# Two attentions in one Trainium2 kernel: V by column tiles, the first K and Q in parts, PE warmed in one run, more clock-keeping matmuls early on

## The chip, the cores and the metric

The kernel runs on one core of one Trainium2 chip. The core has four engines that matter here, each with an instruction stream of its own, tied together by semaphores: TensorE (PE, with its weight loads PEld), VectorE (DVE), ScalarE (ACT) and GpSimd (POOL). SyncE (SP) issues DMAs. The metric is the device time of one execution in microseconds, as the median of several runs; lower is better.

## What is computed

Two independent layers read different inputs, and their outputs stand side by side in the last axis. Part A is attention of 16 query heads over one shared key and value head; part B is attention of 16 heads, each query over the 8 keys at distances 0, 2, ... 14 behind it.

```python
S, D, H, Dh = 2048, 448, 16, 28
# A: x (1,S,D), wq (D,D), wk and wv (D,Dh), wo (D,D)
q = (x @ wq).reshape(B, S, H, Dh).transpose(0, 2, 1, 3)
k = x @ wk;  v = x @ wv
p = softmax(einsum("bhqd,bkd->bhqk", q, k) * Dh ** -0.5)
a = einsum("bhqk,bkd->bhqd", p, v).transpose(0, 2, 1, 3).reshape(B, S, D) @ wo
# B: x (1,S,D), wqkv (D,3D), wo (D,D); W = 8, dil = 2
idx = pos[:, None] - 2 * arange(8)[None, :]
logits = einsum("bhsd,bhswd->bhsw", q, k[:, :, idx]) * Dh ** -0.5   # -1e9 where idx < 0
b = einsum("bhsw,bhswd->bhsd", softmax(logits), v[:, :, idx]).transpose(...).reshape(B, S, D) @ wo
out = concatenate([a, b], axis=-1)
```

## The kernel before

**Part A in units.** The queries are cut into four chunks of 512 (`sc`), the heads into four groups of four (`t`, head `j` of a group on 32 partitions of its own), the keys into 16 blocks of 128 (`tb`). A unit is one (sc, t, tb, j): scores of 128 keys by 512 queries. There are 1024 units, 64 to a (sc, t), which the code calls a quad (a "group" in the text below). PSUM banks 0 to 4 are a ring of two slots, one of three banks and one of two, so a round of both slots takes five units. For each slot PE makes the scores, ACT takes the exp of the whole slot in one instruction (1536 or 1024 columns, `expT`, L833), and PE multiplies four exps at a time with V (L879, output on 32 partitions for each j, bank 5). Scores have two forms: four heads' worth of 32-row tiles side by side (L816), or full 128-row matmuls against `kz`, a copy of K that is zero outside the rows of head j (L813).

In some rounds of each group one unit is not done by ACT: DVE computes its exp by a polynomial, a conversion for each unit (`d_x`, L912) and three steps for each pair of units (L921, L923, L925, 1024 columns each) that leave `dexp`. `OFF_AT` lists these rounds for each group.

**The head.** The first two chunks of x are loaded by ACT's queue in rows (`stage`, also `xst`) and transposed by PE (`a_tr`, L694) and copied to `xT_A` (L702 on DVE, L705 on ACT); the other two come by transposing DMAs (L608). From `xT_A` come K of each chunk (L660), Q of each group (L752) and V of each chunk (L716). K and Q carry their own squared norm: a Square of the projection (ACT L758 and L666 for the first, DVE L670/L672 and L762/L764 for the others), a matmul with `hq` that adds it (L674, L766), and an add of a column on DVE that leaves `kT` (L677) and `qT` (L770). V is scaled by `gcol`, an exp of a column of K (L723 on PE, L727 on ACT, L731 on DVE), and lands in `v_aug`, with its factor copied in by POOL (L729). Before all this PE runs `WARM` matmuls on zeros (L651) that nobody reads.

**Part B** works through 16 blocks of 128 queries (`b_qk` L1003, `b_v` L1018, `b_logits` L1044 and L1053, `b_soft`, `b_out` L1098 to L1114) with PSUM banks 6 and 7, which it shares with the later K, Q, V and with A's output projection (L962).

**The order is planned.** Every instruction is entered with an estimated duration, its reads and writes, a rank `pr` (lower goes first) and an earliest time `rel`, in planned microseconds. A list scheduler (`Sched.run`) walks the engines' clocks and always starts the ready instruction of the lowest rank; the result is a fixed order for each engine, with semaphore waits between engines. What it does not see is the true time: an engine that meets an unfulfilled wait stands, with all that is behind it.

```python
if limit is not None and not o.ring and not (o.pv and npv > self.NPV) and T + o.dur > limit + self.EPS - (0 if o.tiled else self.MODE):
    nxt = limit if nxt is None else min(nxt, max(limit, T + 0.02))
    continue
key = (o.pr, o.idx)
```

`limit` is the time when the next scores or conversion of the ring are due, so other work is only put where it fits ahead of them. The planner also counts the columns that PE got in the last `WIN` microseconds, `area(T)`, and where the count is low it adds matmuls on zeros, the clock-keeping matmuls (L413 in a free bank, L436 next to small matmuls, L808 in a ring slot), or gives scores their full form (L813). `WANT`, `IDLE`, `FULL` and `LOW` are the thresholds:

```python
elif (o.full and area(T) < (self.FULL[o.full] if T + 0.22 * o.full + 0.2 <= H + self.EPS else self.LOW)
      and all(d.start is not None and d.end + self.lat(d) <= T for d in o.opt)):
    o.dur = 0.22 * o.full
```

`H` is the planned time at which ACT runs out of exps.

## Time and profile before

| | us |
|---|---|
| median of 8 runs | 453.22 (452.18 to 456.26) |
| the profiled execution: its own time | 452.85 |
| its span, first to last instruction | 450.8 |
| busy in the span: ACT, PE, DVE | 435.3, 419.5, 417.1 |
| first exp of the ring starts | 11.72 |
| last exp ends (chain: 443.57 and 1.46 more) | 445.03 |
| granted TensorE clock, mean | 0.996 |

A row of the profile's groups has the line of the code, the engine, the operation, output and inputs by name with their shapes, the count, then busy time and mean duration in ns, and last the idle time of the engine just before such instructions with what ended it. A row of a timeline starts with the start and the length in us of the merged instructions. The chain is the work that ended last, followed backwards; its share of the span by engine says which engine sets the end. Durations of matmuls include their run through the array, so that back-to-back ones overlap in the record.

### The profile page before, as it was taken

How to read it: one execution, taken by the hardware profiler on the slowest of the kernel's cores; microseconds unless marked ns; L12 is line 12 of the kernel's file. 1: busy time of each engine (PE TensorE's matmuls, PEld its weight loads, DVE VectorE, ACT ScalarE, POOL GpSimd, SP SyncE). 2: the span in 40 equal slices, each digit the busy share in tenths (PEclk: the TensorE clock that was granted, in tenths of full speed). 3: DMA queues.
4: the chain of work that ended last, by engine and by line, in shares of the span. 5: the costliest groups of instructions: out<-in, count | busy, mean ns of one | idle time of the engine just before them, and what ended most of it. 6: DMA issues, size and time to landing. Idle time of an engine off the chain costs nothing.

```text
span 450.8 us, 9035 instructions
## 1 busy us (share of the span) xinstructions
PE 419.5 (93%) x3806; PEld 164.9 (37%) x3806; DVE 417.1 (93%) x672; ACT 435.3 (97%) x429; POOL 14.4 (3%) x37
## 2 busy tenths in 40 slices
...
PEclk9999999999999999999999999999999999999998
...
DMA packets 39988, 27.30 MB, mean 61 GB/s; under 512 B 15518, under 2 KB 39592, under 8 KB 39948
## 3 DMA queue, kind: packets, MB, share of 16 engines
...
q0 software_dynamic: 816, 1.53, 1.9%
...
q14 instruction: 10, 0.08, 0.1%
...
## 4 chain that ended last, share of the span: by engine, by line
ACT 91%; DVE 4%; PE 3%; DMA 1%; issue 0%
ACT expT L833 90%; DMA stage<-in_A_x_dram 1%; PE ps L660 1%; DVE kz L680 1%; DVE d_x L912 1%; ACT e_t L1079 1%; DVE d_u L921 1%; DVE d_u L923 1%; PE ps L694 0%; PE ps L813 0%; DVE qT L770 0%; DVE kT L677 0%; PE ps L436 0%; DVE xT_A L702 0%; PE ps L816 0%; DVE kT L670 0%
## 5 line engine op out<-in xcount | busy, mean ns | idle before, releaser
L833 ACT ACTIVATE expT<-ps 128x1024 bf16<-128x1024 f32 (+1 forms) x410 | 429.8, 1261 | 4.1 <-PE ps L816 1.9
L816 PE MATMUL ps<-qT,kT 32*128 32x512 bf16 (+1 forms) x918 | 130.4, 372 | 13.7 <-ACT expT L833 10.6
L879 PE MATMUL ps<-expT,v_aug 128*32 128x512 bf16 (+1 forms) x1000 | 89.8, 375 | 1.4 <-ACT expT L833 1.0
L816 PEld LDWEIGHTS ps<-qT,kT 32*128 32x128 bf16 x918 | 32.8, 91 | 101.7 <-ACT expT L833 87.0
L912 DVE TENSOR_SCALAR d_x<-ps 128x512 f32<-128x512 f32 x84 | 57.6, 685 | 2.1 <-PE ps L816 1.9
L813 PE MATMUL ps<-qT,kz 128*128 128x512 bf16 (+1 forms) x170 | 47.2, 368 | 7.1 <-ACT expT L833 5.5
L925 DVE SCALAR_TENSOR_TENSOR dexp<-d_u,d_x 128x1024 int16<-128x1024 f32 x42 | 51.3, 1221 | 0.1
L923 DVE SCALAR_TENSOR_TENSOR d_u<-d_u,d_x 128x1024 f32<-128x1024 f32 x42 | 51.2, 1220 | 0.1
L921 DVE SCALAR_TENSOR_TENSOR d_u<-d_x 128x1024 f32<-128x1024 uint16 x42 | 51.2, 1218 | 0.2
L1044 DVE TENSOR_TENSOR stage<-qTB,kTB 112x1024 bf16<-112x1024 bf16 x64 | 42.5, 681 | 1.0 <-PE ps L1053 0.9
L1104 PE MATMUL ps<-ident,prod 128*112 128x128 bf16 x512 | 42.2, 224 | 0.0
L1098 DVE TENSOR_TENSOR prod<-Vsh,a_n 128x896 bf16<-128x896 bf16 x64 | 37.7, 620 | 4.7 <-PE ps L1104 4.7
L1003 PE MATMUL ps<-xT_B,wqkv 128*128 128x512 bf16 x128 | 39.0, 384 | 0.7 <-DVE qT L770 0.4
L879 PEld LDWEIGHTS ps<-expT,v_aug 128*32 128x32 bf16 x1000 | 22.0, 93 | 47.9 <-issue 43.1
L1104 PEld LDWEIGHTS ps<-ident,prod 128*112 128x112 bf16 x512 | 34.0, 130 | 14.7 <-issue 11.7
L1053 PEld LDWEIGHTS ps<-ones,stage 112*128 112x128 bf16 x512 | 19.9, 96 | 9.2 <-issue 4.3
L1053 PE MATMUL ps<-ones,stage 112*128 112x4 bf16 x512 | 22.9, 167 | 0.0
L752 PE MATMUL ps<-xT_A,wq 128*128 128x512 bf16 x64 | 19.8, 385 | 0.3 <-DVE kTB L1008 0.2
L813 PEld LDWEIGHTS ps<-qT,kz 128*128 128x128 bf16 x170 | 10.9, 97 | 24.0 <-ACT expT L833 21.1
L1018 PE MATMUL ps<-wqv,xT_B 128*128 128x448 bf16 x64 | 18.1, 356 | 0.9 <-DVE kTB L1008 0.5
L1111 PE MATMUL ps<-wo_B,oT 112*128 112x448 bf16 x64 | 18.3, 357 | 0.0
L962 PE MATMUL ps<-wo,oTn 128*128 128x448 bf16 x64 | 16.6, 357 | 1.1 <-DVE oTn L948 1.1
...
## 6 DMA issues: line engine op xcount, KB each, us to landing
...
```

The lines of the kernel that those rows point to most:

```text
L813: r = e.matmul(g.bank(b0 + i, nq, nq * k), g.kz[:, j, 128 * tb:128 * tb + 128], g.qT[:, sc % 2, t, q0:q0 + nq], start=True, stop=True)
L816: r = e.matmul(g.bank(b0 + i, nq, nq * k), g.kT[32 * j:32 * j + 32, 128 * tb:128 * tb + 128], g.qT[32 * j:32 * j + 32, sc % 2, t, q0:q0 + ...
L833: x = a("act", t_exp(w), lambda e, b0=b0, w=w, n=n: e.activation(g.expT[:, n % ERING, 0:w], g.ps[:, 512 * b0:512 * b0 + w], ACT.Exp, scale ...
L879: x = e.matmul(g.bank(PVBANK, nq, q0, p0=32 * j, p1=32 * j + 32), g.v_aug[:, w, tb, :], src[:, nq * k:nq * k + nq], start=first, stop=last ...
L912: o = a("dve", t_dve_ps(512), lambda e: e.tensor_scalar(out=xx[:, 512 * h:512 * h + 512], in0=g.bank(bank), scalar1=-128.0 * A2, scalar2=1 ...
L921: a("dve", t_dve_1x(1024), lambda e: e.scalar_tensor_tensor(out=u, in0=lo, scalar=EP * F, in1=lo, op0=ALU.add, op1=ALU.mult), R=di, W=["d_ ...
L923: a("dve", t_dve_1x(1024), lambda e: e.scalar_tensor_tensor(out=v, in0=u, scalar=EQ * F * F, in1=lo, op0=ALU.add, op1=ALU.mult), R=["d_u"] ...
L925: a("dve", t_dve_1x(1024), lambda e: e.scalar_tensor_tensor(out=out, in0=v, scalar=EL / F ** 3, in1=xx, op0=ALU.mult, op1=ALU.subtract), R ...
L1003: a("pe", t_mm(512), lambda e, u=u, t=t, kt=kt, w=w: e.matmul(g.bank(u.bank), g.wqkv[:, kt, w * D + KC * t:w * D + KC * t + 128], g.xT_B[: ...
L1044: op = a("dve", t_dve_2x(1024), lambda e, t=t, qv=qv, kv=kv: e.tensor_tensor(out=g.prodT[0:KC, t, :, :], in0=qv, in1=kv, op=ALU.mult), R=R ...
L1053: r = e.matmul(g.bank(u.bank, 128).rearrange("p (h w) -> p h w", w=WIN)[:, 4 * t:4 * t + 4, w], g.prodT[0:KC, t, w, :], g.ones4[:, :], sta ...
L1104: a("pe", 0.056, lambda e, u=u, t=t, w=w: e.matmul(g.bank(u.bank, 128, 128 * t, p1=KC), g.prod2[:, w, KC * t:KC * t + KC], g.ident[:, :], ...
```

## The change

- The warming matmuls become one planned instruction of eight with the first rank of PE, and a ninth not before 4.6.
- K of chunk 0 and Q of the first group are made in two parts of 256 columns, each with a Square, a norm matmul and an add of its own. Scores of key blocks 0 and 1 need only the first part of K (`key_of`).
- V turns its operands round: `wv4` (32 columns wide) is the stationary side, x streams by in four column tiles at a time, and DVE transposes the result (`vT`) before the scaling. The `gcol` column goes into K's bank.
- The first group's DVE units come in rounds 4 to 7 instead of 7 to 10. The polynomial steps get a rank that grows with the group (`pp`: -25 for the first, 1.7 for the second, 26.7 more for each further one) in place of -1.5, and `d_x` has three buffers.
- The DVE steps of Q of the first chunk get rank -2.
- `area` counts 200 less between 14 and 50, and thresholds, weights and some durations of the plan are set anew.
- B starts not before 30; late loads are issued later (`wqv` 15, `wo_B` 40, `wo4` 44, the third and fourth chunk of `xT_B` 60 and 130); the rest of `wq` and the zero rows of V's scratch go earlier.

```diff
-WARM = 9
+WARM = 8
+KF = 256
...
-OFF_AT[0] = (7, 8, 9, 10)
+OFF_AT[0] = (4, 5, 6, 7)
 LATE = 2
-PSTT = -1.5
+PSTT = -35.0
 DR = 2
+DX = 3
...
-    MODE = 0.09
+    MODE = 0.096
...
-    WIN = 2.2
-    WANT = 1200.0
-    IDLE = 1300.0
-    FULL = {2: 1500.0, 3: 1200.0}
-    LOW = 900.0
-    QKT = 0.315
+    WIN = 2.5
+    WANT = 1300.0
+    IDLE = 1400.0
+    FULL = {2: 1400.0, 3: 1300.0}
+    LOW = 1200.0
+    QKT = 0.32
...
-            return sum(d for (t1, d) in recent if t1 > T - self.WIN) / self.WIN
+            return sum(d for (t1, d) in recent if t1 > T - self.WIN) / self.WIN - (200.0 if 14 < T < 50 else 0.0)
...
-                if ok and left > 40:
+                if ok and left > 10:
...
+                elif mode and not o.tiled:
+                    o.dur += o.extra
...
-        self.d_x = sb([128, 2, 1024], FP32, "d_x")
+        self.d_x = sb([128, DX, 1024], FP32, "d_x")
...
-        self.outA = sb([128, 4, D], BF16, "outA")
+        self.outA = sb([128, 2, D], BF16, "outA")
...
+        a("dve", 0.1, lambda e: e.memset(g.wv4[:, :, :], 0.0), W=["wv4z"], pr=-6.5)
...
-        a("gp", 0.5, lambda e: e.memset(g.Vst[:, 0, :], 0.0), W=[("Vst", 0)], pr=-8.05)
...
-        a("gp", 1.5, wload(g.wq, g.A_wq, KC, D), R=[("d_x", 0, 0), ("d_x", 0, 1)], W=[("wq", 1)], dsem="i_wq", land=4, pr=-7.5, ninc=2)
+        a("gp", 1.5, wload(g.wq, g.A_wq, KC, D), R=[("d_x", 0, 0), ("d_x", 0, 1)], W=[("wq", 1)], dsem="i_wq", land=5.5, pr=-8.15, ninc=2)
...
-                    transpose=True)), R=[("xst", 0)], W=[("xT", c, t)], dsem=f"i_xa{c}.{t}", land=3.8, pr=-20 + c)
+                    transpose=True)), R=[("xst", 0)], W=[("xT", c, t)], dsem=f"i_xa{c}.{t}", land=5.0 if c == 2 else 8.0, pr=-20 + c)
...
-                    transpose=True)), R=[("xst", 0)], W=[("xT_B", c, t)], dsem=f"i_xb{c}.{t}", land=4.5, pr=-16 + c)
+                    transpose=True)), R=[("xst", 0)], W=[("xT_B", c, t)], dsem=f"i_xb{c}.{t}", land=6.0, pr=-16 + c, rel=(0, 0, 60, 130)[c])
...
-          W=["wqv"], dsem="i_wbv", land=5, pr=-7, ninc=2)
+          W=["wqv"], dsem="i_wbv", land=8, pr=-7, rel=15, ninc=2)
...
-            for t in range(4)], W=["wo_B"], dsem="i_wob", land=5, pr=2, rel=4, ninc=4)
+            for t in range(4)], W=["wo_B"], dsem="i_wob", land=5, pr=2, rel=40, ninc=4)
...
-            for j in range(4)], W=["wo4"], dsem="i_wo4", land=5, pr=2, rel=4, ninc=4)
...
+            for j in range(4)], W=["wo4"], dsem="i_wo4", land=5, pr=2, rel=44, ninc=4)
+        a("sp", 0.6, one(lambda e: e.dma_start(out=g.v_dram[0:PAD, :], in_=g.warm[0:PAD, 0:D])),
+          R=["warm"], W=[("vd", -1)], dsem="i_vz", land=2.5, pr=-24)
...
+        a("dve", 0.1, lambda e: e.tensor_copy(out=g.wv4[:, :, 0:DH], in_=g.wv[:, :, :]), R=["wv", "wvz", "wv4z"], W=["wv4"], pr=-5)
...
+    VPR = 0.5
+    VP0 = 0.5
+    BREL = 30.0
...
-        for i in range(WARM):
-            u = Use(f"warm{i}", (3,))
-            a("pe", 0.33, lambda e, u=u: e.matmul(g.bank(u.bank), g.warm[:, 0:128], g.warm[:, :], start=True, stop=True),
-              R=["warm"], use=u, pr=-15)
+        for n, pr, rel in ((WARM, -30, 0.0), (1, -15, 4.6)):
+            def warm(e, n=n):
+                for _ in range(n):
+                    r = e.matmul(g.bank(3), g.warm[:, 0:128], g.warm[:, :], start=True, stop=True)
+                return r
+            u = Use(f"warm{n}", (3,))
+            a("pe", 0.43 * n, warm, R=["warm"], use=u, pr=pr, rel=rel)
         for c in range(NCH):
             pr = -9 if c == 0 else c
             HB = g.HB if c == 0 else g.LB
             if c < 2:
                 g.a_tr(c)
-            u = Use(f"K{c}", HB, late=c == 0)
-            for kt in range(4):
-                a("pe", t_mm(512), lambda e, u=u, c=c, kt=kt: e.matmul(
-                    g.bank(u.bank), g.wk4[:, kt, :], g.xT_A[:, kt, 512 * c:512 * c + 512],
-                    start=kt == 0, stop=kt == 3),
-                  R=[("xT", c, kt), "wk4"], W=[u], use=u, pr=pr, rel=8.0 * min(c, 1), dense=512)
-            ksq = g.k_sq[:, c % 2, :]
-            if c == 0:
-                a("act", t_act(512), lambda e, u=u, ksq=ksq: e.activation(ksq, g.bank(u.bank), ACT.Square),
-                  R=[u, "d_u"], W=[("k_sq", c % 2)], use=u, pr=-100)
-            else:
-                kc = g.kT[:, 512 * c:512 * c + 512]
-                a("dve", t_dve_ps(512), lambda e, u=u, kc=kc: e.tensor_copy(out=kc, in_=g.bank(u.bank)),
-                  R=[u], W=[("kT", c)], use=u, pr=min(pr, -2))
-                a("dve", t_dve_2x(512), lambda e, ksq=ksq, kc=kc: e.tensor_tensor(out=ksq, in0=kc, in1=kc, op=ALU.mult),
-                  R=[("kT", c), "d_u"], W=[("k_sq", c % 2)], pr=-2)
-            a("pe", t_mm(512), lambda e, u=u, ksq=ksq: e.matmul(g.bank(u.bank), g.hq[:, 2, :], ksq, start=False, stop=True, skip_group_check=True),
-              R=[("k_sq", c % 2), "hq", "d_u"], W=[u], use=u, pr=pr, dense=512)
+            for k, (lo, n) in enumerate(((0, KF), (KF, 512 - KF)) if c == 0 else ((0, 512),)):
+                u = Use(f"K{c}.{k}", HB, late=c == 0)
+                for kt in range(4):
+                    a("pe", t_mm(n), lambda e, u=u, c=c, kt=kt, lo=lo, n=n: e.matmul(
+                        g.bank(u.bank, n), g.wk4[:, kt, :], g.xT_A[:, kt, 512 * c + lo:512 * c + lo + n],
+                        start=kt == 0, stop=kt == 3),
+                      R=[("xT", c, kt), "wk4"], W=[u], use=u, pr=pr + 0.1 * k, rel=8.0 * min(c, 1), dense=n)
+                ksq = g.k_sq[:, c % 2, lo:lo + n]
+                kc = g.kT[:, 512 * c + lo:512 * c + lo + n]
+                if c == 0:
+                    a("act", t_act(n), lambda e, u=u, ksq=ksq, n=n: e.activation(ksq, g.bank(u.bank, n), ACT.Square),
+                      R=[u, "d_u"], W=[("k_sq", c % 2, k)], use=u, pr=-100)
+                else:
+                    a("dve", t_dve_ps(n), lambda e, u=u, kc=kc, n=n: e.tensor_copy(out=kc, in_=g.bank(u.bank, n)),
+                      R=[u], W=[("kT", c, k)], use=u, pr=min(pr, -2))
+                    a("dve", t_dve_2x(n), lambda e, ksq=ksq, kc=kc: e.tensor_tensor(out=ksq, in0=kc, in1=kc, op=ALU.mult),
+                      R=[("kT", c, k), "d_u"], W=[("k_sq", c % 2, k)], pr=-2)
+                a("pe", t_mm(n), lambda e, u=u, ksq=ksq, n=n: e.matmul(
+                    g.bank(u.bank, n), g.hq[:, 2, :], ksq, start=False, stop=True, skip_group_check=True),
+                  R=[("k_sq", c % 2, k), "hq", "d_u"], W=[u], use=u, pr=pr + 0.1 * k, dense=n)
+                a("dve", t_dve_ps(n) + 0.08, lambda e, u=u, kc=kc, n=n: e.tensor_scalar(
+                    out=kc, in0=g.bank(u.bank, n), scalar1=g.cols[:, 0:1], scalar2=None, op0=ALU.add),
+                  R=["kadd"], W=[("kT", c, k)], use=u, pr=min(pr, -2) - (1 - k if c == 0 else 0))
             kc = g.kT[:, 512 * c:512 * c + 512]
-            a("dve", t_dve_ps(512), lambda e, u=u, kc=kc: e.tensor_scalar(
-                out=kc, in0=g.bank(u.bank), scalar1=g.cols[:, 0:1], scalar2=None, op0=ALU.add),
-              R=["kadd"], W=[("kT", c)], use=u, pr=min(pr, -2))
-            g.kz_ops[c] = [a("dve", Lock(0.265), lambda e, j=j, c=c, kc=kc: e.tensor_scalar(
+            g.kz_ops[c] = [a("dve", Lock(0.3), lambda e, j=j, c=c, kc=kc: e.tensor_scalar(
                 out=g.kz[:, j, 512 * c:512 * c + 512], in0=kc, scalar1=g.cols[:, 8 + j:9 + j], scalar2=None, op0=ALU.mult),
-                R=["jmask", ("kT", c)], W=[("kz", c)], pr=4 + c) for j in range(4)]
+                R=["jmask"] + g.keys_of(c), W=[("kz", c)], pr=4 + c) for j in range(4)]
             if c == 0:
                 g.a_q(0, first=True)
-            g.a_v(c)
+            g.a_v(c, u)
+
+    def key_of(self, tb):
+
+        return ("kT", tb // 4, int(KF <= 128 * tb < 512))
+
+    def keys_of(self, c):
+        return sorted({self.key_of(4 * c), self.key_of(4 * c + 3)})
...
+    def a_v(self, c, uk):
+
+        g, a = self, self.s.add
+        pr = c + (g.VPR if c else g.VP0)
+        u = Use(f"V{c}", g.LB)
+        for kt in range(4):
+            def vm(e, u=u, kt=kt):
+                for i in range(4):
+                    r = e.matmul(g.bank(u.bank, 128, 0, 32 * i, 32 * i + 32), g.wv4[:, kt, :],
+                                 g.xT_A[:, kt, 512 * c:512 * c + 512].rearrange("p (t i e) -> p i t e", t=4, e=32)[:, i],
+                                 start=kt == 0, stop=kt == 3, tile_position=(0, 32 * i))
+                return r
+            o = a("pe", 0.13, vm, R=[("xT", c, kt), "wv4"], W=[u], use=u, pr=pr, rel=11.0 if c == 0 else 0, dense=192)
+            o.tiled = True
+        a("dve", t_dve_ps(128), lambda e, u=u: e.transpose(out=g.vT[:, c % 2, :], in_=g.bank(u.bank, 128)),
+          R=[u], W=[("vT", c % 2)], use=u, pr=-2)
+        u = uk
...
             a("pe", 0.06, lambda e, u=u, b=b, tb=tb: e.matmul(
-                g.bank(u.bank, 1, 128 + b), g.kT[0:32, 128 * tb:128 * tb + 128], g.e30[:, :], start=True, stop=True),
-              R=[("kT", c), "e30"], W=[u], use=u, pr=pr)
+                g.bank(u.bank, 1, b), g.kT[0:32, 128 * tb:128 * tb + 128], g.e30[:, :], start=True, stop=True),
+              R=g.keys_of(c) + ["e30"], W=[u], use=u, pr=pr)
...
         a("dve", Lock(0.15), lambda e: e.tensor_scalar(
             out=g.v_aug[:, 1, 4 * c:4 * c + 4, :], in0=g.v_aug[:, 0, 4 * c:4 * c + 4, :], scalar1=-2.0 ** EOFF, scalar2=None,
-            op0=ALU.mult), R=[("v_aug", 0, c), ("v_aug1", 0, c)], W=[("v_aug", 1, c), ("v_aug1", 1, c)], pr=pr + 4)
+            op0=ALU.mult), R=[("v_aug", 0, c), ("v_aug1", 0, c)], W=[("v_aug", 1, c), ("v_aug1", 1, c)], pr=-1.6)
...
+            for hf, (lo, n) in enumerate(((0, 256), (256, 256)) if first and t == 0 else ((0, 512),)):
+                pr += 0.1 * hf
+                u = Use(f"Q{sc}.{t}.{hf}", banks, late=first and t == 0)
+                for kt in range(4):
+                    a("pe", t_mm(n), lambda e, u=u, t=t, kt=kt, lo=lo, n=n: e.matmul(
+                        g.bank(u.bank, n), g.wq4[:, t, kt, :], g.xT_A[:, kt, 512 * sc + lo:512 * sc + lo + n],
+                        start=kt == 0, stop=kt == 3),
+                      R=[("xT", sc, kt), ("wq4", t)], W=[u], use=u, pr=pr, rel=rel, dense=n)
...
+                if first and t == 0:
+                    a("act", t_act(n), lambda e, u=u, qs=qs, n=n: e.activation(qs, g.bank(u.bank, n), ACT.Square),
+                      R=[u], W=[k1], use=u, pr=-100)
+                else:
...
+                      R=[u], W=[k2], use=u, pr=-2 if first else -1)
+                    a("dve", t_dve_2x(n), lambda e, qs=qs, qt=qt: e.tensor_tensor(out=qs, in0=qt, in1=qt, op=ALU.mult),
+                      R=[k2], W=[k1], pr=-2 if first else -1)
...
+                a("dve", t_dve_ps(n) + 0.06, lambda e, u=u, qt=qt, n=n: e.tensor_scalar(
+                    out=qt, in0=g.bank(u.bank, n), scalar1=g.cols[:, 1:2], scalar2=None, op0=ALU.add),
+                  R=["qadd"] + ([("qTh", 0)] if n < 512 and hf else []), W=[("qTh", 0) if n < 512 and not hf else k2],
+                  use=u, pr=pr if first and t == 0 else -2 if first else -1)
...
-            o.dense = 128
+            o.dense = 256 + 32 * len(us)
...
-        o = a("pe", 0.315 if len(qd) == 2 else 0.42, pv, R=sorted({y[1] for y in grp}) + sorted(
-            {(k, y[3], z[0] // 4) for k in ("v_aug", "v_aug1") for y in grp for z in g.parts(y[0])}), pr=-40, dense=700)
+        o = a("pe", 0.332 if len(qd) == 2 else 0.42, pv, R=sorted({y[1] for y in grp}) + sorted(
+            {(k, y[3], z[0] // 4) for k in ("v_aug", "v_aug1") for y in grp for z in g.parts(y[0])}), pr=-40, dense=768)
...
+            pp = 10.0 + 26.7 * (4 * g.quad[0] + g.quad[1]) + PSTT
             u, v = g.d_u[:, :], g.d_v[:, :]
             lo = xx.bitcast(mybir.dt.uint16).rearrange("p (c two) -> p c two", two=2)[:, :, 0]
-            di = [("d_x", m % 2, 0), ("d_x", m % 2, 1)]
+            di = [("d_x", m % DX, 0), ("d_x", m % DX, 1)]
             a("dve", t_dve_1x(1024), lambda e: e.scalar_tensor_tensor(
-                out=u, in0=lo, scalar=EP * F, in1=lo, op0=ALU.add, op1=ALU.mult), R=di, W=["d_u"], pr=PSTT)
...
-            ob = blk % 4
+            ob = blk % 2
...
-                rel = T - 22 + 2.5 * i if c == 0 else T - 60 + 6 * i
+                rel = max(g.BREL, T - 22 + 2.5 * i) if c == 0 else T - 60 + 6 * i
...
-        rel = T - 6
+        rel = max(T - 6, g.BREL)
...
-                a("pe", 0.1, lgs, R=[("prodT", t), "ones4"], W=[u], use=u, pr=pr)
```

## The prediction

> **What bounds the kernel now.** I read the shares of busy time and the chain on the page first, then the waits of ACT, ACT's instructions in order of time, and last the chain and the DVE and PE instructions of the two places where ACT stands idle.
>
> ```profile
> PE 419.5 (93%) x3806; PEld 164.9 (37%) x3806; DVE 417.1 (93%) x672; ACT 435.3 (97%) x429; POOL 14.4 (3%) x37
> PEclk9999999999999999999999999999999999999998
> ACT 91%; DVE 4%; PE 3%; DMA 1%; issue 0%
> L833 ACT ACTIVATE expT<-ps 128x1024 bf16<-128x1024 f32 (+1 forms) x410 | 429.8, 1261 | 4.1 <-PE ps L816 1.9
> ```
>
> PE, DVE and ACT are each busy for 93 to 97% of the span, but the chain is ACT for 91% of it, and nearly all of that is one line, the 410 exps of L833. What counts is when the first one starts, how long ACT stands between them, and what follows the last. The row of L833 gives 4.1 us of idle in all. The waits of ACT, and ACT in order of time, say where:
>
> ```profile
> ACT expT L833 <- PE ps L816: 1.9, 1, 1.9
> ACT expT L833 <- PE ps L813: 1.5, 1, 1.5
> ACT expT L833 <- PE ps L879: 0.7, 1, 0.7
> ...
> 8.35 0.60 ACT L758 ACTIVATE q_sq<-ps 128x512 bf16<-128x512 f32 x1 [1.46 <-PE ps L752]
> 9.22 0.60 ACT L666 ACTIVATE d_u<-ps 128x512 bf16<-128x512 f32 x1 [0.27 <-PE ps L660]
> 11.72 5.97 ACT L833 ACTIVATE expT<-ps 128x1536 bf16<-128x1536 f32 x5 [1.91 <-PE ps L816]
> ...
> 33.39 5.11 ACT L833 ACTIVATE expT<-ps 128x1024 bf16<-128x1024 f32 x5 [0.66 <-PE ps L879]
> ...
> 40.32 8.29 ACT L833 ACTIVATE expT<-ps 128x1024 bf16<-128x1024 f32 x8 [1.48 <-PE ps L813]
> ```
>
> 1.91 us of the 4.1 lie before the first exp (11.72), 0.66 before the one at 33.39 and 1.48 before the one at 40.32. After 40.32 the view shows no wait of an exp on anything. So ACT can win 11.7 us of head, 2.1 us of holes, and 5.8 us of tail (the last exp ends at 445.03 in the chain, the span at 450.8); the rest is exp work. The second column of the fence is the time of the merged row, so 8.35 and 9.22 are the Squares of Q and K.
>
> ```profile
> 4.80 1.89 PE L694 MATMUL ps<-ident,stage 128*128 128x128 bf16 x16 [0.38 <-DMA stage<-in_A_x_dram]
> 6.91 0.55 PE L752 MATMUL ps<-xT_A,wq 128*128 128x512 bf16 x1
> 7.29 0.38 PE L651 MATMUL ps<-warm 128*128 128x512 bf16 x1
> 7.51 0.81 PE L752 MATMUL ps<-xT_A,wq 128*128 128x512 bf16 x3
> 8.15 1.03 PE L660 MATMUL ps<-xT_A,wk 128*128 128x512 bf16 x4
> ...
> 37.40 0.42 DVE L764 TENSOR_TENSOR q_sq<-qT 128x512 bf16<-128x512 bf16 x1
> 37.73 1.22 DVE L923 SCALAR_TENSOR_TENSOR d_u<-d_u,d_x 128x1024 f32<-128x1024 f32 x1
> 38.87 0.75 DVE L770 TENSOR_SCALAR qT<-ps,cols 128x512 bf16<-128x512 f32 x1
> 39.71 1.22 DVE L925 SCALAR_TENSOR_TENSOR dexp<-d_u,d_x 128x1024 int16<-128x1024 f32 x1
> ```
>
> The first five lines are PE in the head: a warming matmul (L651 at 7.29) stands between the first and second Q matmuls (L752), which had their inputs by 7.14. The last four are DVE ahead of the hole at 40.32: the steps of Q for the second head group (q_sq at L764, qT at L770) lie between the 1.22 us steps of the exp polynomial (L923, L925).
>
> **The change, part by part.** The sum is made against the profiled execution, 452.85 us (span 450.8 and 2.05 around it). It is 0.37 below the median of the eight runs, 453.22; I count the result from 452.85. A difference of 0.5%, 2.3 us, is about what a measurement of this kernel can tell from none.
>
> *Exp work: 0.* OFF_AT[0] keeps four rounds, at 4 to 7 instead of 7 to 10, so ACT has the same number of exps of 1024 and of 1536. The 429.8 us of L833 stay.
>
> *Head, Q and K in two halves, one warming run: -1.1.* Before, Q's matmuls end at 8.32 (chain), Square at 8.95, K's Square at 9.82, qT 9.49 to 10.24, a copy of the second x chunk for 0.33, kT to 11.23, first exp 11.72. Now the last xT copy is at 7.14 as before. Without the matmul at 7.29, Q's first half (256 columns, half of 0.216 each) with its drain is through at about 7.7, allowing for the second half's matmuls between. Square of 256: 0.60 less 0.21 (the rows of 1024 and 1536 show 0.83 ns for a column) is 0.38, so 8.1 and, for the second half, 8.5. The L813 matmul of 256 takes 0.275, so the norms are in at 8.4 and 8.8. The add on DVE is 0.75 for 512; the transpose L939 falls from 710 to 447 ns when halved, so 0.48: 8.95 and 9.4. K's first half: Square to 8.9, norm 9.2, add behind Q's to 9.85. Scores, then exp 0.43 later as now (11.29 to 11.72): 10.3. The copy of 0.33 that got in between now may do so again: 10.6, or -1.1. Ends: -1.7 (no copy, halves fully staggered) and +0.3 (four adds where there were two, and a copy before both).
> Is one long warming run worth more? In the trace, the 16 transposes at 4.80 take 1.89 us, about 107 ns apart, and the last eight before the first scores (10.10) take 0.61 us. So PE came to its full pace only near 7.2, 6 us after its first matmul at 1.25. [...] I take 0 and keep 0.8 for the low end. The ninth matmul (not before 4.6) costs 0.43 ahead of Q only if x is late; x copies cover it.
>
> *V by column tiles: 0.* Before: 16 matmuls of 28 columns per chunk (L716), some 28 ns apart (ten in 0.42), and four of L723. Now 16 of 128 columns in four sets of four. L879, the same tiling, runs four matmuls of 512 in 0.40 and eight in 0.62, so a set of 512 costs 0.22 and of 128 some 0.06: 0.24 against 0.45 per chunk, on an engine that is not the bound. [...] The row does not bear a loss out: L879 loads 32 columns in 93 ns where L716 loads 128 in 96, and there are 16 loads either way. [...] DVE gets four transposes of 128 columns, between 0.2 and 0.3 each, about 1 us of a DVE that has 3.8 us idle between 20 and 30 in the windows view; with that cover gone, chunk 3's kT (below) is later by as much.
>
> *The two holes: -2.1.* At 33.4, PE's next attention-times-V (L879) waited for v_aug of chunk 2 (DVE L731 at 32.62), whose V matmuls had been strewn from 27.3 to 30.3 at a low rank. They are now four instructions of a better rank: -0.66. At 40.3 the wait was for qT (L770 ends 39.63). Its DVE steps now rank ahead (-2 instead of 3.8), and the polynomials come three rounds, about 3 x 2.23 = 6.7 us, sooner (1330 and 903 ns for the two exps of a round), so they are done by 31: -1.48.
>
> *What is late next: +0.5.* The early polynomials meet K of chunk 3. Its keys are due after 48 units, 9.6 rounds: 5.6 full ones of 2.23 and four with one unit moved off, 1.81 each (two exps of 903 ns), 19.7 us after 10.6, less 1.3 for the scores ahead: 29.0. Before it was ready at 28.22 (L677 27.47 for 0.75), with no polynomial before 30.88. Now its three DVE steps can each find a polynomial step of 1.22 in front, as q_sq and qT did. Ready between 28.8 and 31: a hole of 0 to 2, and I take 0.5 since it needs two of three.
>
> *More clock-keeping matmuls: +0.3.* area() is lowered by 200 between 14 and 50, so more L436/L413 kind of matmuls go out and more scores take the L813 form. One costs 0.22 of PE. PE idles 2.6 us of these 36 in the windows view. In the windows view the granted clock is 1.00 throughout these 36 us, so there is no slow stretch to win back in this execution: 0 to +5.8 (rival 3), and I take one score held.
>
> *Other stages, all 0 with +-1.5:* the largest recorded hole, 1.48, is the bound. A third d_x buffer and evacuations ahead of polynomials from the second group on can take away small waits or make them. B: its Q and K not before 30, but their first matmul was at 40.98 anyway; they now rank behind Q of groups three and four, 2 x 1.9 us of DVE, covered by B's last output, at 438 before a last exp at 445; without that cover +2. SP: the zero rows of V go first, in the pause from 1.9 to 4.77; two chunks of xT_B go later, needed after 60. POOL: wq earlier; wqv to 15, wo_B and wo to 40 and 44 (4.9 us of issuing), first needed at 130.9 and 135. The last gcol copy, on POOL at 38.90, is ahead of them; if it slipped past 40 it would wait up to 4.9. The outA ring of two has 1.7 us landings against turns 2 us apart or more. Tail: one more 0.22 matmul at most, beside DVE's work.
>
> Sum: -1.1 - 2.1 + 0.5 + 0.3 = -2.4, so 450.4.
>
> **Rivals.** (1) *Gain given back*: K of chunk 3 late by the full 2.0 takes the place of the hole at 40.3. For it: DVE is at 9.96 of 10 us from 30 to 40, and all its work stays. Against: 1.2 and 3.8 us of DVE idle in 14 to 20 and 20 to 30 (windows view). 452.85 - 3.2 + 2.0 + 0.3 = 451.9. (2) *More*: full pace early (0.8), no copy (0.3), no new hole, 0.8 of small waits gone: 452.85 - 3.2 - 1.9 = 447.8. (3) *Slower*: keeping matmuls in front of scores. From 14 to 50 there are 36/2.23 = 16 rounds, 32 scores. A forced one in front of scores with no slack (exps of 903 ns leave 0.9 less 0.39 for scores and the release) holds ACT by 0.22 plus a change of tiling, about 0.1. Eighteen held cost 5.8: 452.85 - 2.7 + 5.8 = 456.0. It decides from nine on. Against: 41 of them today stand in gaps, and ACT shows no wait for one. (4) *The change does not do what it says*: the warming run warms nothing, since full pace comes at 7.2 as before. My sum has it so; it takes nothing off.
>
> **Numbers.** Main case 0.46 (449.2 to 451.7 by itself), rival 1 0.21, rival 2 0.17, rival 3 0.16. Faster by over 0.5%, below 450.95: 0.38 of the main case, all of rival 2, 0.02 of rival 1: 0.57. Same: 0.28. Slower: 0.15. Range 447.4 to 455.2: it leaves out half of rival 3 and little below.
>
> **What would show it.** First exp at 10.3 to 10.9; exps 410 with the same forms; no hole at 33 and 40, at most one near 28 to 31 released by L677 or L813; L651 in one block from 1.25 and one more before Q. Wrong: a first exp after 11.4; ACT waits over 2 us between 14 and 50, or behind a clock-keeping matmul; a hole after 50; weight loads of V that stand end to end.

## Result and the profile after

The changed kernel takes 450.53 us in the median of 20 runs (450.24 to 453.62), beside 453.42 us for the kernel before, measured with it (57 runs, 452.07 to 457.88). The ratio is 0.9934, with a 95% interval from 0.9915 to 0.9952: faster by 0.5 to 0.85%. The prediction was 450.4, range 447.4 to 455.2.

The profiled execution of the changed kernel is not one of its usual ones. Its own time is 452.15 us (span 450.4), while 8 of the 20 runs lie between 450.24 and 450.25. What made it longer is seen below; a run with the same order up to the last microseconds (`a_tail`) stands beside it wherever the difference matters.

The page of the changed kernel, with the lines that answer to those shown of before:

```profile
PE 420.7 (93%) x3807; PEld 159.5 (35%) x3807; DVE 418.0 (93%) x680; ACT 435.8 (97%) x431; POOL 14.0 (3%) x36
ACT 93%; PE 5%; DVE 2%; DMA 0%; issue 0%
L864 ACT ACTIVATE expT<-ps 128x1024 bf16<-128x1024 f32 (+1 forms) x410 | 430.8, 1322 | 3.5 <-PE ps L847 2.4
```

Busy times are as before (ACT 435.8 against 435.3, and the exps, now L864, 430.8 against 429.8). The chain is ACT for 93%. So the exp work did not change, as the prediction had it, and the question stays when the first exp starts, where ACT stands, and what follows the last exp. The waits of ACT (total, times, longest):

```profile
ACT outA L1001 <- DMA out_dram<-outA: 3.6, 1, 3.6
ACT expT L864 <- PE ps L847: 2.4, 3, 1.2
ACT expT L864 <- PE ps L844: 0.9, 2, 0.5
```

ACT in order of time (start, length, and in brackets the idle time before with its releaser):

```profile
10.52 1.45 ACT L864 ACTIVATE expT<-ps 128x1536 bf16<-128x1536 f32 x1 [1.18 <-PE ps L847]
12.79 4.63 ACT L864 ACTIVATE expT<-ps 128x1536 bf16<-128x1536 f32 x4 [0.75 <-PE ps L847]
17.90 2.37 ACT L864 ACTIVATE expT<-ps 128x1024 bf16<-128x1024 f32 x2 [0.48 <-PE ps L847]
21.67 1.02 ACT L864 ACTIVATE expT<-ps 128x1024 bf16<-128x1024 f32 x1 [0.42 <-PE ps L844]
23.19 3.00 ACT L864 ACTIVATE expT<-ps 128x1024 bf16<-128x1024 f32 x3 [0.49 <-PE ps L844]
```

The first exp starts at 10.52 instead of 11.72. The holes of before at 33.39 and 40.32 are gone: after 23.19 the view has no wait of an exp, up to the end of the stretch read, 50 us, and the five waits above add up to all that the waits view gives to exps (3.3). In the place of the old holes stand four new ones, all early: 0.75, 0.48, 0.42 and 0.49. The last two are this execution's own. The windows view of the changed kernel has (window, length, then busy time of PE, PEld, DVE, ACT and POOL, the granted clock of PE, DMA share, GB/s):

```profile
20.00:24.00 4.00, 3.79 (x21) 0.84 (x21) 2.36 (x8) 3.09 (x5) 0.20 (x1) 0.57 1.47 163
```

PE was busy for 3.79 of these 4 us, at a granted clock of 0.57. In steps of half a us the view has 0.50 from 20.5 to 23.5, 0.58 to 24 and 1.00 before and after, so 4 x 0.43 / 0.5 = 3.4 us at half pace. Two wide scores (L844) took 1.03 us there. `a_tail`, whose order is the same here, has clock 1.00 in this window and ACT busy for all 4 us. Its ACT in order of time:

```profile
10.12 1.45 ACT L864 ACTIVATE expT<-ps 128x1536 bf16<-128x1536 f32 x1 [1.18 <-PE ps L847]
12.39 4.62 ACT L864 ACTIVATE expT<-ps 128x1536 bf16<-128x1536 f32 x4 [0.75 <-PE ps L847]
17.50 2.37 ACT L864 ACTIVATE expT<-ps 128x1024 bf16<-128x1024 f32 x2 [0.48 <-PE ps L847]
```

The views show no wait of an exp after that. With it the 2.6 us come out as a sum (each term from the start of the first exp, the end of the last, the span and the run's own time):

| us | before | after | `a_tail` |
|---|---|---|---|
| first exp starts | 11.72 | 10.52 | 10.12 |
| first exp to the end of the last | 433.30 | 433.49 | 432.05 |
| end of the last exp to the end of the span | 5.78 | 6.39 | 6.33 |
| outside the span | 2.05 | 1.75 | 1.75 |
| own time | 452.85 | 452.15 | 450.25 |

`a_tail`'s 450.25 is also the usual time of the changed kernel. So an undisturbed execution gains 1.6 at the head, 1.25 between the exps (2.14 of old holes gone, 1.23 of new ones, and a rest of 0.34: 0.19 less of ACT's busy time there, 430.91 to 430.72, and 0.15 of small pauses) and 0.3 outside the span, and loses 0.55 in the tail.

The time outside the span goes with the parts of K and Q. The nine kernels of this study that have them, `c_best` apart, lie at 1.74 to 1.78 us in the median, the four that have them whole (before, `b_V`, `b_off4`, `a_whole`) at 2.06 to 2.10; the runs of `c_best`, with parts, spread from 1.79 to 2.40. Why is not known.

The tail is mostly DVE's. DVE of the kernel before, DVE of the changed kernel, then its ACT, in order of time:

```profile
446.01 0.20 DVE L944 RECIPROCAL rden<-PV_T 128x8 f32<-128x8 f32 x1
446.25 0.43 DVE L945 TENSOR_TENSOR oN<-PV_T,rden 128x256 bf16<-128x256 f32 x1
...
445.19 0.21 DVE L976 RECIPROCAL rden<-PV_T 128x8 f32<-128x8 f32 x1
445.31 0.58 DVE L1004 CAST outA<-ps 128x448 bf16<-128x448 f32 x1
445.81 0.41 DVE L977 TENSOR_TENSOR oN<-PV_T,rden 128x256 bf16<-128x256 f32 x1
...
447.61 0.54 ACT L1001 ACTIVATE outA<-ps 128x448 bf16<-128x448 f32 x1 [3.60 <-DMA out_dram<-outA]
```

Before, oN came 0.24 us after the reciprocal's start (446.01 to 446.25); now 0.62, since a copy to outA (L1004, 0.58) stands between them. That is 0.38. PV_T starts 0.69 after the last exp instead of 0.50, another 0.19: PE's last multiplication with V starts 0.24 after that exp (444.25) instead of 0.04, behind a run of five matmuls of the output projection (L994 at 442.93). Together 0.57. ACT's last copy waits 3.60 us, which the view puts down to the DMA that has to leave outA, now a ring of two.

### The profile page after: what moved, and what is told of

It reads as the page before. It is cut to its first block, busy times and chain, and to the rows that moved or that the text cites. A ratio compares the mean times of both kernels' runs of the same rounds, so it can differ in the third digit from the quotient of the medians.

```text
span 450.4 us, 9056 instructions
## 1 busy us (share of the span) xinstructions
PE 420.7 (93%) x3807; PEld 159.5 (35%) x3807; DVE 418.0 (93%) x680; ACT 435.8 (97%) x431; POOL 14.0 (3%) x36
## 4 chain that ended last, share of the span: by engine, by line
ACT 93%; PE 5%; DVE 2%; DMA 0%; issue 0%
ACT expT L864 92%; PE ps L663 1%; PE ps L844 1%; PE ps L910 1%; PE ps L847 1%; ACT e_t L1111 0%; PE ps L717 0%; DVE kT L692 0%; DMA out_dram<-outA 0%; PE ps L675 0%; DVE kz L696 0%; DVE qT L800 0%; PE ps L839 0%; PE ps L781 0%; PE ps L1085 0%
## 5 line engine op out<-in xcount | busy, mean ns | idle before, releaser
L864 ACT ACTIVATE expT<-ps 128x1024 bf16<-128x1024 f32 (+1 forms) x410 | 430.8, 1322 | 3.5 <-PE ps L847 2.4
L847 PE MATMUL ps<-qT,kT 32*128 32x512 bf16 (+1 forms) x1043 | 152.7, 371 | 17.0 <-ACT expT L864 12.3
L910 PE MATMUL ps<-expT,v_aug 128*32 128x512 bf16 (+1 forms) x1000 | 94.8, 377 | 0.4 <-DVE PV_T L971 0.4
L847 PEld LDWEIGHTS ps<-qT,kT 32*128 32x128 bf16 x1043 | 38.2, 91 | 117.4 <-ACT expT L864 104.3
L1136 PE MATMUL ps<-ident,prod 128*112 128x128 bf16 x512 | 47.2, 226 | 0.0
L910 PEld LDWEIGHTS ps<-expT,v_aug 128*32 128x32 bf16 x1000 | 24.2, 93 | 54.2 <-issue 50.9
L1085 PE MATMUL ps<-ones,stage 112*128 112x4 bf16 x512 | 20.3, 167 | 0.0
L1085 PEld LDWEIGHTS ps<-ones,stage 112*128 112x128 bf16 x512 | 17.3, 96 | 8.1 <-issue 5.4
L781 PE MATMUL ps<-xT_A,wq 128*128 128x512 bf16 (+1 forms) x68 | 19.7, 371 | 0.0
L994 PE MATMUL ps<-wo,oTn 128*128 128x448 bf16 x64 | 17.3, 357 | 1.7 <-DVE oTn L980 1.6
L1035 PEld LDWEIGHTS ps<-xT_B,wqkv 128*128 128x128 bf16 x128 | 9.8, 97 | 18.3 <-issue 12.2
L971 DVE STREAM_TRANSPOSE PV_T<-ps 128x512 f32<-128x512 f32 (+1 forms) x17 | 11.6, 682 | 4.8 <-PE ps L910 4.8
```

The lines of the kernel that those rows point to most:

```text
L847: r = e.matmul(g.bank(b0 + i, nq, nq * k), g.kT[32 * j:32 * j + 32, 128 * tb:128 * tb + 128], g.qT[32 * j:32 * j + 32, sc % 2, t, q0:q0 + ...
L864: x = a("act", t_exp(w), lambda e, b0=b0, w=w, n=n: e.activation(g.expT[:, n % ERING, 0:w], g.ps[:, 512 * b0:512 * b0 + w], ACT.Exp, scale ...
L910: x = e.matmul(g.bank(PVBANK, nq, q0, p0=32 * j, p1=32 * j + 32), g.v_aug[:, w, tb, :], src[:, nq * k:nq * k + nq], start=first, stop=last ...
L1035: a("pe", t_mm(512), lambda e, u=u, t=t, kt=kt, w=w: e.matmul(g.bank(u.bank), g.wqkv[:, kt, w * D + KC * t:w * D + KC * t + 128], g.xT_B[: ...
L1085: r = e.matmul(g.bank(u.bank, 128).rearrange("p (h w) -> p h w", w=WIN)[:, 4 * t:4 * t + 4, w], g.prodT[0:KC, t, w, :], g.ones4[:, :], sta ...
L1136: a("pe", 0.056, lambda e, u=u, t=t, w=w: e.matmul(g.bank(u.bank, 128, 128 * t, p1=KC), g.prod2[:, w, KC * t:KC * t + KC], g.ident[:, :], ...
```

## Experiments

**The theory and its rivals.** The theory: the gain is that of the order, since the parts of K and Q bring the first exp forward, V by column tiles and the ranks close the two holes, and the clock-keeping adds nothing. One rival: the new clock accounting makes it, by sparing PE slow windows. Another: the early head alone makes it, and the rest is beside the path.

One caution holds for all. Every edit changes the input of the list scheduler, and so the whole order behind it; a part undone also shuffles what comes later. A difference of about 1 us between two kernels is therefore not the price of the one edit unless the trace shows the place. The column "fastest" stands for the executions least touched by slow PE windows (mean granted clock 0.997 to 1.000 in each of them); ratios are to the kernel before on the same chip in the same sitting.

| kernel | edit | median us (runs) | fastest | ratio, 95% | first exp |
|---|---|---|---|---|---|
| after | | 450.53 (20) | 450.24 | 0.9934 [0.9915, 0.9952] | 10.52 |
| a_tail | last outputs get buffers of their own | 450.30 (14) | 450.19 | 0.9962 [0.9945, 0.9979] | 10.12 |
| a_area0 | without the 200 less between 14 and 50 | 451.13 (22) | 449.22 | 0.9956 [0.994, 0.9973] | 10.18 |
| a_oldclock | all clock accounting as before | 449.65 (6) | 449.61 | 0.9931 [0.9909, 0.9953] | 10.06 |
| a_gcol | gcol of chunk 0 in a bank of its own | 451.82 (15) | 450.45 | 0.9974 [0.9958, 0.999] | 10.06 |
| a_oldV | all of `a_v` as before | 457.47 (7) | 455.08 | 1.0087 [1.0051, 1.0123] | 10.70 |
| a_whole | first K and Q in one part | 452.08 (12) | 452.00 | 0.9972 [0.9949, 0.9995] | 10.86 |
| a_off7 | OFF_AT as before | 452.44 (12) | 451.71 | 0.9979 [0.9954, 1.0004] | 10.06 |
| a_warm9 | nine warming matmuls as before | 451.88 (12) | 450.65 | 0.9971 [0.9957, 0.9984] | 10.06 |
| b_V | before, with the new `a_v` | 452.86 (12) | 450.87 | 0.9972 [0.9949, 0.9996] | 11.22 |
| b_halves | before, with K and Q in parts | 455.14 (12) | 453.01 | 1.0037 [1.0013, 1.0061] | 10.16 |
| b_off4 | before, with early polynomials and ranks | 453.63 (12) | 452.62 | 1.0025 [0.9996, 1.0055] | 11.57 |
| c_best | the best pieces together | 449.97 (6) | 449.43 | 0.9932 [0.9915, 0.9949] | 10.07 |

The fastest runs of the kernel before were 452.03, 452.06 and 452.10 in the three sittings.

### V by column tiles, and the parts of K and Q

`a_oldV`: `a_v` as before, all else as changed. This puts back more than the operands: the rank of V and gcol is 1.3 again instead of 0.5, gcol lies in V's bank, and the second, scaled half of `v_aug` has rank c + 5.3 instead of -1.6.

```diff
-        u = Use(f"V{c}", g.LB)
-        for kt in range(4):            # wv4 stationary, four column tiles
+        u = Use(f"V{c}", g.LB, spare=160)
+        for b in range(4):             # x stationary, 28 columns of wv, pr = c + 1.3
```

> The changed kernel with V as before: 16 matmuls of 28 columns with x stationary for each chunk, no transposes on DVE, gcol in V's bank (so the second scores no longer wait for ACT's gcol). Theory 1 (V is worth nothing by itself, only its place in the order counts): the hole at 12.8 goes and others come, within 0.5 of 450.5. Rival (the 16 single matmuls per chunk crowd PE between 14 and 41 when the DVE units come early): holes of 2 us or more between 14 and 45, 452 or above.

ACT in order of time, and PE's matmuls with V (L906 here):

```profile
10.70 8.29 ACT L860 ACTIVATE expT<-ps 128x1536 bf16<-128x1536 f32 x7 [1.18 <-PE ps L843]
18.88 0.17 ACT L750 ACTIVATE gcol<-ps 128x4 f32<-128x4 f32 x1
20.25 5.60 ACT L860 ACTIVATE expT<-ps 128x1024 bf16<-128x1024 f32 x6 [1.19 <-PE ps L906]
30.22 5.22 ACT L860 ACTIVATE expT<-ps 128x1024 bf16<-128x1024 f32 x5 [2.21 <-PE ps L906]
...
19.79 1.05 PE L906 MATMUL ps<-expT,v_aug 128*32 128x512 bf16 x16
```

The first exp is at 10.70. The exps go to seven buffers in turn (`ERING`), and a buffer is free again when PE has multiplied it with V. After the seventh exp (10.70 to 18.99) ACT waits 1.19 for that. At 19.79 PE has sixteen matmuls with V in a row where the changed kernel has four or eight: they had piled up. The matmuls that make V were over by 16.27 (L739); what came late is gcol, which ACT read at 18.88, so that `v_aug` was done on DVE at 19.35 (13.95 in `a_tail`), and three wide scores stood ahead on PE. ACT waits 2.21 at 30.22, again for L906, and 1.99 at 27.84 for a gcol whose PE columns (L746) are strewn between 25.18 and 27.62, with clock-keeping matmuls between them. The granted clock is 0.52 from 24 to 31 in this execution, so part of the last two waits is the clock's; the fastest run, at a mean clock of 0.998, has no room for such a stretch and is still 4.8 us above the changed kernel's fastest (6.9 between the medians). It is the largest effect of the study, and it belongs to the whole of `a_v`; the term that the prediction set at 0. Which of the operands, the ranks and gcol's place makes it, no run separates.

`b_V`: the kernel before with only the new `a_v`: V turned round, the new ranks, and gcol in a bank of its own.

```diff
+        for kt in range(4):
+            a("pe", 0.13, vm, ...)     # vm: four column tiles of 128, one set
+        a("dve", t_dve_ps(128), lambda e, u=u: e.transpose(out=g.vT[...], in_=g.bank(u.bank, 128)), ...)
```

> The kernel before with V by column tiles alone (gcol in a bank of its own out of 6 and 7, V's rank as in the changed kernel); K and Q whole, warming, DVE units and accounting as before. The runs so far: without V by column tiles the changed kernel is at 457.5, with holes behind PE's attention-times-V and gcol. Theory 1 now (V by column tiles frees PE between 14 and 41 and is what closes the holes): first exp as before, 11.1 to 11.8, holes before 41 under 1 us in all where there were 2.1, so 450.5 to 451.5. Rival (V only pays with the earlier head): 452 to 452.8.

ACT in order of time:

```profile
11.22 2.37 ACT L843 ACTIVATE expT<-ps 128x1536 bf16<-128x1536 f32 x2 [1.91 <-PE ps L826]
18.38 2.37 ACT L843 ACTIVATE expT<-ps 128x1536 bf16<-128x1536 f32 x2 [0.21 <-PE ps L826]
```

This is all that ACT waits for an exp here: 1.91 before the first, 0.21 once more before 50. The new `a_v` closes both holes by itself, with `OFF_AT` and the rank of Q as before; its ranks and gcol's bank changed along with the operands, so the turning alone is not shown to do it. The first exp is 0.5 earlier with Q and K whole, which is PE's pace in the head (the 16 transposes take 1.42 us where before had 1.89), as below. Its runs divide: five at 450.87 to 451.14, the others from 452.71 up, so the ratio is only 0.9972.

`b_halves`: the kernel before with only K and Q in two parts.

```diff
-            u = Use(f"K{c}", HB, late=c == 0)
+            for k, (lo, n) in enumerate(((0, KF), (KF, 512 - KF)) if c == 0 else ((0, 512),)):   # KF = 256
```

> The kernel before with one part of the change: K of chunk 0 and Q of the first group in two parts of 256 columns, scores of key blocks 0 and 1 waiting for the first part of K alone. Warming, V, DVE units and the clock accounting are as before. Theory 1 (the head gains by the halves): first exp 0.8 to 1.2 us earlier than before at a like time of full PE pace, so about 10.6. Whether the end gains as much depends on the holes behind, which this leaves: if the holes are a matter of K, V and Q being late and not of the first exp, they grow by what the head won, and the time stays at 452 to 452.8. Rival (the head decides alone): 451.2 to 451.6.

ACT in order of time, and one row of PE:

```profile
10.16 8.49 ACT L847 ACTIVATE expT<-ps 128x1536 bf16<-128x1536 f32 x7 [0.85 <-PE ps L830]
20.02 5.54 ACT L847 ACTIVATE expT<-ps 128x1024 bf16<-128x1024 f32 x5 [1.30 <-PE ps L893]
35.16 4.20 ACT L847 ACTIVATE expT<-ps 128x1024 bf16<-128x1024 f32 x4 [2.53 <-PE ps L893]
...
34.71 0.83 PE L893 MATMUL ps<-expT,v_aug 128*32 128x512 bf16 x12 [0.89 <-DVE v_aug L741]
```

The first exp is at 10.16, 1.56 earlier (some of it pace: the transposes take 1.68 us instead of 1.89), and the kernel is slower than before: the matmuls with V (L893) now come before V is ready (0.89 for v_aug at 34.71, twelve matmuls behind it), and ACT waits 1.30 and 2.53 for them. The rival of the head alone falls: an early first exp is worth nothing if V cannot follow.

`a_whole`: the changed kernel with K and Q whole.

```diff
-KF = 256
+KF = 512
...
-            for hf, (lo, n) in enumerate(((0, 256), (256, 256)) if first and t == 0 else ((0, 512),)):
+            for hf, (lo, n) in enumerate(((0, 512),)):
```

> The changed kernel with K of chunk 0 and Q of the first group whole again (512 columns), and so no part of the scores ready earlier; one long warming run, V by column tiles, early DVE units, ranks and accounting stay. Theory 1: first exp about 1.0 us later than the changed kernel's, at 11.1 to 11.5, and the time 0.7 to 1.1 us up, 451.0 to 451.5. Rival (holes that follow absorb it, since K and V of the later chunks set the pace there): 450.2 to 450.6.

First exp at 10.86, later holes 0.42, 0.49, 0.69 and 0.49, fastest 452.00. So the parts are worth 0.80 at the first exp at a like pace (10.86 less the 10.06 of `a_oldclock`; the transposes take 1.07 us in both), and 1.8 in the fastest runs. Against `a_tail` these 1.8 are 0.74 before the first exp, 0.65 between the exps and 0.35 outside the span.

### Warming

`a_warm9`: nine separate warming matmuls, as before.

```diff
-        for n, pr, rel in ((WARM, -30, 0.0), (1, -15, 4.6)):
+        for i in range(WARM):                              # WARM = 9
```

> The changed kernel with nine separate warming matmuls of rank -15, as before. In the profiles so far PE came to full pace at 7.2 (before), 6.9, 6.0, 6.0, 5.2, 4.4 and 4.0 us, whatever the warming. [...] Rival (the one run brings full pace sooner): full pace after 7 us, first exp at 11 or later, 451 or more.

First exp at 10.06, with the holes of `a_tail` and one more of 0.82 at 40.61. The transposes of the first chunk in four kernels, from PE in order of time. The changed kernel:

```profile
4.84 1.89 PE L717 MATMUL ps<-ident,stage 128*128 128x128 bf16 x16
```

`a_tail`, with the same instructions:

```profile
4.65 1.72 PE L717 MATMUL ps<-ident,stage 128*128 128x128 bf16 x16
```

`a_warm9`:

```profile
4.82 1.07 PE L714 MATMUL ps<-ident,stage 128*128 128x128 bf16 x16 [0.40 <-DMA stage<-in_A_x_dram]
```

`a_oldclock`, the same in this stretch as the changed kernel, with the first Q matmuls behind:

```profile
4.66 1.07 PE L717 MATMUL ps<-ident,stage 128*128 128x128 bf16 x16
6.32 1.16 PE L781 MATMUL ps<-xT_A,wq 128*128 128x256 bf16 x8 [0.38 <-DVE wq L645]
```

Sixteen transposes take 1.89 us at half pace and 1.07 at full; in the changed kernel those sixteen start some 107 ns apart, the later ones of the head (from 8.87 on) 56. (The windows view gives a granted clock of 1.00 for 4 to 7 us in all four, so the pace of the head is read from the durations alone.) The changed kernel is at half pace to nearly the end, `a_tail` a little less, `a_oldclock` and `a_warm9` (seven matmuls one by one) are at full pace. The kernel before, with seven one by one, was at half pace. So the form of the warming run does not decide it, and the same form gives different answers. What does decide it, no run shows. But full pace by 4.8 brings only 0.06 over full pace by 6.0 (10.06 against 10.12): then Q waits for DVE's copy of its weights (wq, L645). The most that the pace gives in this order is 10.52 less 10.06, 0.46 and not 0.8.

### Clock accounting

`a_area0` drops the 200, `a_oldclock` all of the new accounting:

```diff
-            return sum(...) / self.WIN - (200.0 if 14 < T < 50 else 0.0)
+            return sum(...) / self.WIN
...                                     # a_oldclock besides, with other weights:
-        self.extra = 0.012
+        self.extra = 0.0
...
-    MODE = 0.096
+    MODE = 0.09
...
-    WIN = 2.5
-    WANT = 1300.0
-    IDLE = 1400.0
-    FULL = {2: 1400.0, 3: 1300.0}
-    LOW = 1200.0
+    WIN = 2.2
+    WANT = 1200.0
+    IDLE = 1300.0
+    FULL = {2: 1500.0, 3: 1200.0}
+    LOW = 900.0
...
-            o.dense = 256 + 32 * len(us)
+            o.dense = 128
```

> The changed kernel without the 200 taken off area() between 14 and 50. Theory 1 (the gain is the earlier first exp and the closed holes before 41): the head stays, first exp at 10.5, so 450 to 451 in executions at the full clock; fewer clock-keeping matmuls matter only if a window at half clock comes more often. Theory 2 (the gain is the clock, kept by those matmuls): the times spread over 3 us as before the change, and the median goes up by 1 us or more, to over 451.5.

> The changed kernel with all of the plan's clock accounting as before: no 200 off, WIN, WANT, IDLE, FULL, LOW, MODE and the weights of the instructions as before, so that scores take their full form (128-row matmuls) some 83 times where the changed kernel has 18. Theory 1: first exp at 10.5, time 450 to 451 as the changed kernel's. Theory 2 (the rest of the span gained by fewer full scores and other thresholds): the steady part loses 1 us or more, 451.5 to 452.5, and ACT's row of exps from 41 to the end is longer than the changed kernel's.

Neither kernel has a hole before 50 beyond the 0.75 and 0.48 of `a_tail`. Without the 200, the fastest runs are 1.0 us faster than the changed kernel's (449.22), but half are not; two windows of its profiled execution:

```profile
138.00:142.00 4.00, 3.03 (x15) 0.72 (x15) 4.00 (x8) 3.65 (x5) 0.00 (x0) 0.64 0.11 33
295.00:299.00 4.00, 3.10 (x12) 0.81 (x11) 2.89 (x7) 2.98 (x4) 0.00 (x0) 0.64 0.00 0
```

The clock falls to 0.64 to 0.68 in places far behind the 50 us that the edit speaks of, and ACT loses 0.35 and 1.02 of 4 us (a third such window is at 264 to 268, clock 0.68). With all of the old accounting, 5 of 6 runs lie within 449.61 to 449.85. The rival of the accounting falls: the gain is there without the new accounting. The order planned without it is even 0.6 faster in the fastest runs (449.61 against 450.24), and more than half of that is one place. DVE of `a_oldclock` near the end:

```profile
440.27 0.62 DVE L1004 CAST outA<-ps 128x448 bf16<-128x448 f32 x1 [0.57 <-PE ps L994]
443.07 0.20 DVE L976 RECIPROCAL rden<-PV_T 128x8 f32<-128x8 f32 x1
443.31 0.42 DVE L977 TENSOR_TENSOR oN<-PV_T,rden 128x256 bf16<-128x256 f32 x1
```

The copy to outA runs ahead of the last chain and not between its steps, and the tail is 5.96 instead of the 6.33 of `a_tail`. The rest is 0.06 at the first exp and 0.22 between the exps. So the 0.6 is no price of the thresholds as such.

The new accounting also brings fewer clock-keepers, against its description: 45 matmuls of wide scores (L844) where the kernel before has 170 and `a_oldclock` 161, and in the first 50 us 7 matmuls on zeros and 9 wide scores where before has 14 and 19. (Over the whole span the records show 56 matmuls on zeros besides the warming, before 65; but `a_tail`, of the same order, shows 46, so too many records are missing to compare these.) The heavier weight of the tiled scores in the count (256 and more in place of 128) may make PE look busier to the planner than it is; that this is what makes `a_area0` unsteady was not tested.

### Polynomials and the rank of Q

`a_off7` takes `OFF_AT[0]` back to (7, 8, 9, 10); `b_off4` gives the kernel before (4, 5, 6, 7), the rank `pp` and the rank -2 for Q:

```diff
-OFF_AT[0] = (4, 5, 6, 7)              # a_off7, against the changed kernel
+OFF_AT[0] = (7, 8, 9, 10)
...
-OFF_AT[0] = (7, 8, 9, 10)             # b_off4, against the kernel before
+OFF_AT[0] = (4, 5, 6, 7)
-PSTT = -1.5
+PSTT = -35.0                          # in pp, as in the change
-                  R=[u], W=[("qT", par, t)], use=u, pr=pr if first else -1)
+                  R=[u], W=[("qT", par, t)], use=u, pr=-2 if first else -1)
```

> The changed kernel with the first group's DVE units in rounds 7 to 10 again. Theory 1 (early units close the hole that came before the second group, 1.48 us before the change): a hole of about 1 to 1.5 us comes back near 37 to 41, with Q of the second group late behind the polynomials, so 451 to 452. Rival (the rank of Q's DVE steps closed it, not the rounds): no hole there, 450 to 450.6.

> The kernel before with the first group's DVE units in rounds 4 to 7, the growing rank of the polynomial steps and rank -2 for the DVE steps of Q of the first chunk; all else as before. If these close the hole before the second group (1.48 us): it is under 0.5 at 40, and others come from V and K being late behind the polynomials: 451.5 to 452.5. If the hole stays: 452 to 453.

In `a_off7` no exp waits between 20 and 50: the hole at 40.3 does not need the earlier rounds. Its loss lies elsewhere (0.83 and 0.82 at 99.69 and 181.18, both behind L910). In `b_off4` the polynomials and ranks without the new V leave ACT standing (in an execution whose granted clock is 0.66 from 16 to 21, which bears on the first two) at 16.84 (0.65), 20.91 (0.92), 28.51 (0.44), 34.65 (0.96) and 42.25 (0.43). The one before the second group falls from 1.48 to 0.43 or 0.96, and new ones come; its fastest run (452.62) gains nothing.

### The bank of gcol

`a_gcol` gives the gcol column of chunk 0 a bank of its own instead of that of K's second part, which is a bank of the ring:

```diff
-        u = uk
+        u = uk if c else Use("G0", g.LB)
```

> The changed kernel with the gcol column of chunk 0 in a bank of its own (6 or 7) instead of the bank of K's second part. In the profile of the changed kernel the second scores of the ring start at 12.35, behind a matmul that waits for ACT's gcol (11.87 to 12.04), and ACT stands 0.75 us from 12.04. If that bank is why, the second scores come at about 10.5 and the hole at 12.8 goes, -0.75 there. The order behind it is planned anew, so a later hole can give it back (K of chunk 3 is the candidate): 449.5 to 451.

The hole of 0.75 after the first exp is gone, and the one of 0.48 as well: no exp waits before 23.24 (0.19). The two had one root. In the changed kernel gcol's bank is one of the slot of two banks, and that slot is not free until ACT has read gcol behind its first exp. PE of the changed kernel, then ACT:

```profile
12.03 0.39 PE L839 MATMUL ps<-warm 128*128 128x512 bf16 x1 [0.22 <-ACT gcol L754]
12.35 0.61 PE L847 MATMUL ps<-qT,kT 32*128 32x512 bf16 x5
17.47 0.60 PE L847 MATMUL ps<-qT,kT 32*128 32x512 bf16 x5
...
16.37 1.05 ACT L864 ACTIVATE expT<-ps 128x1024 bf16<-128x1024 f32 x1
```

The exps at 10.52 and 12.79 both have 1536 columns, those at 16.37 and 17.90 both 1024: the slot of three banks is used twice running, and later the slot of two. In `a_gcol` and in the kernel before they alternate. A slot used twice running gets its next scores only when its exp has ended, and ACT stands meanwhile. The scores at 17.47 start 0.05 after the exp that ended at 17.42, and with their 0.43 that is the hole of 0.48. At 12.03 a clock-keeping matmul (L839) goes first and the scores follow at 12.35, so the other hole is 0.32 longer. (The view puts the wait of L839 down to gcol, but it starts 0.01 before that read ends, at 12.04, and 0.06 after the exp, at 11.97.) That the planner chose this order because of the bank is argued from `a_gcol`.

But the order behind it has new ones. The longest, from ACT in order of time:

```profile
39.28 1.02 ACT L864 ACTIVATE expT<-ps 128x1024 bf16<-128x1024 f32 x1 [1.12 <-PE ps L847]
```

The windows view around it:

```profile
39.00:43.00 4.00, 4.00 (x17) 1.22 (x15) 2.45 (x6) 2.49 (x3) 0.00 (x0) 0.57 0.18 49
```

Half pace again, with waits of 1.12 ahead and 1.00 behind (42.56), and a fastest run of 450.45 even without such a window. The cause of the two holes is shown; the gain from closing them is not.

### The tail, and a version of the best pieces

`a_tail` writes the last two outputs from buffers of their own:

```diff
+            ot, ok = (g.outB, "outB") if last else (g.outA, "outA")
-                a("act", t_act(D), lambda e: e.activation(g.outA[:, ob, :], ...), W=[("outA", ob)], ...)
+                a("act", t_act(D), lambda e: e.activation(ot[:, ob, :], ...), W=[(ok, ob)], ...)
```

> The changed kernel, with the last two blocks of A's output copied into B's two output buffers, which are free by then, instead of the ring of two outA buffers. Nothing ahead of the tail moves. In the profile of the changed kernel the last ACT copy stands for the landing of an outA write (447.58), about 0.45 us after its matmuls were done. If the smaller ring costs the tail, 0.4 to 0.5 us go: about 450.1 at the median, -0.7% of the kernel before becoming -0.75%, and no wait of ACT's outA on a DMA. If the tail ends with something else (the order of DVE's steps), nothing moves: 450.5.

The longest wait of ACT now:

```profile
ACT outB L1002 <- PE ps L994: 3.3, 1, 3.3
```

The wait of 3.6 for the DMA is now one of 3.3 for the last projection, and the gain is 0.05 (450.24 to 450.19), a tenth of what was expected. The copy ends 3.87 after the last exp instead of 4.14, but its write lands 1.9 us after its issue instead of 1.7: DVE's write now goes out 0.11 before it and not 0.37. A long wait named at the end of a chain need not be worth its length. The copy between rden and oN was left as it was.

`c_best` joins the old accounting, the bank for gcol, the tail, a later V of chunk 0, rounds (4, 5, 7, 10), and the copy of block 13 on ACT. What it has besides the edits shown:

```diff
-    VP0 = 0.5
+    VP0 = 1.3
-OFF_AT[0] = (4, 5, 6, 7)
+OFF_AT[0] = (4, 5, 7, 10)
-            if last and s4 % 2:
+            if (last and s4 % 2) or (sc, s4) == (3, 1):
```

> The changed kernel with what the runs point to: the clock accounting as before the change (449.65 in an earlier run), gcol of chunk 0 in a bank of its own, V's rank in chunk 0 1.3 instead of 0.5, the first group's DVE units in rounds 4, 5, 7 and 10, the last but two copies of A's output on ACT, which is idle then, instead of between DVE's last steps, and the last two in B's output buffers. Expected: no hole at 12.8, last exp 0.4 earlier than with the old accounting alone, tail 0.4 to 0.5 shorter: 448.4 to 449.2. If the order planned anew leaves windows at half clock, the median is over 450.

Its fastest run is 449.43, its median 449.97: inside the spread of `a_oldclock`, and above what was expected. The hole at 12.8 is gone, as expected; the tail is 5.95, no shorter than that of `a_oldclock`. Its trace waits 0.65 at 17.67 and 1.15 at 40.13, the latter behind a stretch at a granted clock of 0.57 (36 to 40). The version to keep is `a_oldclock`: 0.65 below `a_tail` in the same sitting (449.65 against 450.30) and 0.6 below the changed kernel's fastest. By the ratios alone the three cannot be told apart (0.9931, 0.9962 and 0.9934, with intervals that overlap), and `a_oldclock` has 6 runs.

## Why the prediction held, point by point

- **Exp work 0:** right (410 exps, 430.8 against 429.8 us).
- **Head -1.1:** measured -1.2 in the trace of after, which has the pace of before (16 transposes in 1.89 us in both), and -1.6 in `a_tail`, 0.4 of it pace. The mechanism was right. The term for an early full pace was 0, with 0.8 kept for the low end and in rival 2. No run shows the 0.8 at the first exp: at full pace the sixteen transposes take 0.82 less (1.07 against 1.89), but the first exp comes only up to 0.46 earlier in this order, from run to run, because Q then waits for its weights.
- **V by column tiles 0:** the step that was mis-sized. It was priced as work on PE and DVE (0.24 against 0.45 a chunk; 0.2 to 0.3 for each of DVE's transposes, measured 0.31), and as work it stayed off the chain. What counts is when `v_aug` is ready: with the early head the new `a_v` as a whole is worth 4.8 to 6.9 us. The -0.66 at 33.4 was put down to V's better rank. `b_V`, which has that rank, the turned operands and a new bank for gcol, closes that hole and the other too; which of the three does it stays open.
- **The two holes -2.1:** both gone. For the one at 40.3 the new `a_v` suffices (`b_V`); the earlier rounds, which the step also named, are not needed (`a_off7`).
- **K of chunk 3, +0.5:** did not come. One polynomial step (1.23 at 29.59) stood in front of its add, kT was ready at 31.47, and no exp waited. The place of the new wait was guessed wrong: 0.75 came at the second scores and 0.48 at 17.90, both from the bank of gcol, at which the step on V did not look.
- **Clock-keeping +0.3:** in size as forecast, one score held: the matmul on zeros at 12.03 puts the second scores 0.32 later, and this is part of the 0.75. It is not one more than before, though. There are fewer early on, and `a_oldclock` has the same hole. Of rival 3's many held scores no other came.
- **Tail and outA, 0:** +0.55. The 0.22 of one matmul at most, which the step allowed, came as 0.19 (the projection in front of the last multiplication with V). What it had wrong is DVE's work beside it: a copy of 0.58 falls between two steps of the last chain and costs 0.38. The ring of two costs 0.05.
- **Rival 1** (451.9) came near by another road: 1.23 + 0.55 were given back, but the head brought 0.5 more, small items 0.34 and the time outside the span 0.3. **Rival 2** (447.8) needed no new hole; no kernel here reached it. **Rival 4** holds as far as the traces go: with one run of eight or single matmuls, full pace comes early in some executions and late in others (1.07 to 1.89 us for the sixteen transposes).

The forecast of -2.4 against the -2.6 found (452.85 to 450.25) is thus partly luck. The new holes, with the held score in them, put on 0.43 more than forecast (1.23 for 0.8), and the tail 0.55. The head (0.5, of which 0.4 is pace), small items (0.34), the time outside the span (0.3) and the old holes (0.04) take 1.18 off. Open are why the parts of K and Q go with a shorter time outside the span, the 0.34 of small items, and why the fastest runs of `a_area0` are 1.0 faster: its tail is 0.36 shorter (5.97 in its trace against 6.33), the rest is not traced.
